# A middle q load on ScalarE's queue, and a new order of turns and copies in the first attention

## The chip, the cores and the metric

The kernel runs on one core of a Trainium2 chip. The metric is the device time of one execution in microseconds; of several executions the median is given. A profiled execution has a time of its own, and a span: the time from its first to its last instruction.

## What is computed

An attention with normalised q and k, for 8 batches of 12 heads, 448 positions and a head dimension of 64, and behind it a two-layer network with a tanh GELU (768 to 2048 to 768) over the 8 x 448 = 3584 rows. All inputs and the output are float32 in memory; the kernel multiplies in bfloat16.

```python
def rmsnorm(x, g):
    return x / np.sqrt(np.mean(x * x, axis=-1, keepdims=True) + 1e-06) * g
q_n, k_n = rmsnorm(q, g_q), rmsnorm(k, g_k)
scores = q_n @ k_n.transpose(0, 1, 3, 2) / np.sqrt(64)
attn = softmax(scores)                       # over the keys
x = (attn @ v).transpose(0, 2, 1, 3).reshape(3584, 768)
out = gelu_tanh(x @ w_in) @ w_out
```

## The kernel before

**Tiles.** Twelve heads are taken in three groups of four, here the first, middle and last group of a batch (c = 0, 1, 2; `NCH` is 3). The two head pairs of a group lie side by side. A q or k tile of a group (`rawq`, `rawk`, loaded by `load`, L115) is 128 partitions x 2 x 7 x 64 float32, 448 KB; the 7 (`NT`) are pieces of 64 positions.

**From q and k to scores.** Five steps lie between a load and the scores: the square (`square`, L154, on ScalarE, GpSimd or VectorE), its sum over the 64 columns (`total`, L167, VectorE), the inverse root (`rsqrt`, L190: on ScalarE a logarithm at L195 and an exponential at L202, L211 or L214), the product with the tile (`normed`, L268, on GpSimd or VectorE), the transposes on TensorE, one for each piece (`turn`, L286), and the copy from PSUM to `qT` or `kT` (`put`, L296; for k times the gain). `t_first` stands for pieces 0 to 3 of a tile and `t_rest` for pieces 4 to 6, so each of these steps can be done in two parts.

**Units.** A unit (`unit`, L324) is one k piece of one group against all of that group's q: four matmuls into one of two PSUM buffers (L333), then one exponential of 128 x 896 on ScalarE (L337). A batch has 21 units; units 0 to 6 belong to the first group, 7 to 13 to the middle, and 14 to 20 to the last. Unit i needs `qT` of its group and the k piece i modulo 7, and its buffer must have been left by the exponential of unit i - 2.

**Products.** `products(b, c, what, lo, hi)` (L368) multiplies the exponentials of pieces lo to hi with ones (`what` 0, the sums of the softmax) or with v (`what` 1). For the first two groups of batch 0 both go to the same two PSUM banks (`oall`) one after the other, or the sums go to two spare banks (`spared`). `turned` (L390) moves the sums from PSUM by two 32x32 block transposes (tile `st`), `recips` (L395) takes reciprocals and spreads them by another one (`rb`), and `quad_x` (L404) multiplies the v products by them into `xT`, the network's input.

**Order.** Nothing is re-ordered by a scheduler: each engine works through its instructions in the order in which the program issues them. For batch 0 that order is written out by hand: `first_attention` (L580) runs the 21 units and issues behind unit i what the list `mid` (L732) holds under i, and ahead of unit i what `side` (L725) holds. `idle(2, warm())` (L263) issues two matmuls whose result nobody uses; they write into a bank of `oall`. Later batches mix the attention of batch b + 1 with the second layer of batch b; the change does not touch them.

**The start.** Loads of the first group are cut: half of q by SyncE's queue and half by ScalarE's, k in two parts (`t_first`, `t_rest`) by SyncE's. ScalarE then issues the small load of `g_k` (L626) and loads its table of functions (L627). The middle and the last group's q and k (L628, L629) and batch 1's loads follow on SyncE's queue in order. GpSimd norms the first pieces of the first q (L690), squares middle q and middle k (L694, L696), issues two loads of v, squares last q and k, and issues four loads of `w_in`. VectorE's `total` of the middle k is the last step before the logarithm of `rsqrt(0, 1)`, which ScalarE runs behind unit 2.

**PSUM tiles of pool `ps_m`.** It has two buffers that rotate: a third tile waits until the readers of the first are done. Targets of `turn`, the roots of the last group (`place`) and the spare banks come from it.

Of the kernel before, what the change touches and what calls it, by code (L numbers as in the profile page):

```python
# [8 lines left out]
F32 = mybir.dt.float32  # L9
# [8 lines left out]
def kernel(  # L18
# [11 lines left out]
    nc = tc.nc  # L30
    B, H, S, D = q.shape
# [6 lines left out]
    P = 128  # L38
# [13 lines left out]
    stp = ctx.enter_context(tc.tile_pool(name="stp", bufs=1))  # L52
    smp = ctx.enter_context(tc.tile_pool(name="smp", bufs=4))
# [16 lines left out]
    def pair(name):  # L70
        rounds.append(rounds.pop(0))
        return rounds[-1]

    def three():
        return len(rounds) == 3
# [24 lines left out]
    rows = consts.tile([D, P], BF16)  # L100
# [14 lines left out]
    def load(b, c, n, parts=1, engs=(nc.sync,)):  # L115
        t = rawqk.tile([P, 2, NT, D], F32, tag=f"raw{n}", name=f"raw{n}")
        src = {"q": q, "k": k}[n]
        raws[n, b, c] = t
        m = 2 // parts
        return [  # L120
            lambda i=i: engs[i].dma_start(
                t[:, i * m:(i + 1) * m].rearrange("p a t d -> p a (t d)"),
                src[b, 4 * c + 2 * i * m:4 * c + 2 * (i + 1) * m].rearrange(
                    "(a r) (p t) d -> (r p) a (t d)", r=2, t=NT
                ),
            )
            for i in range(parts)
        ]

    def loads(b, c):  # L130
        for n in "qk":
            for go in load(b, c, n):
                go()
# [15 lines left out]
    def squares(b, c, n, hs, ts):  # L149

        sq = sqs[n, b, c]
        return sq[hs.start][:, :, ts] if type(sq) is list else sq[:, hs, ts]
# [10 lines left out]
    def seat(b, c):  # L163

        return (0, 2, 1)[c] if b == 1 else c

    def total(b, c, n, hs=both, ts=slice(0, NT)):  # L167
        if b not in sss:
            sss[b] = smp.tile([P, NCH, 2, 2, NT], F32, tag="ss", name="ss")
        nc.vector.reduce_sum(  # L170
            sss[b][:, seat(b, c), "qk".index(n), hs, ts], squares(b, c, n, hs, ts), axis=AX.X
        )
# [90 lines left out]
    def idle(n, w):  # L263

        for _ in range(n):
            nc.tensor.matmul(w, filler[:, :128], filler, start=True, stop=True)  # L266

    def normed(b, c, n, eng, ts=slice(0, NT)):  # L268
        if (n, b, c) not in nrms:
            nrms[n, b, c] = nrmp.tile([P, NT, 2, D], BF16, tag=f"nrm{n}", name=f"nrm{n}")  # L270
        m = ts.stop - ts.start
        root = rinvs[b][:, seat(b, c), "qk".index(n)] if eng is nc.gpsimd else roots[n, b, c]
        eng.tensor_mul(  # L273
            nrms[n, b, c][:, ts].rearrange("p t a d -> p a t d"),
            raws[n, b, c][:, :, ts],
            root[:, :, ts].to_broadcast([P, 2, m, D]),
        )

    def qT_of(b):
        if b not in qT:  # L280
            qT[b] = qkp.tile([128, NCH, NT, 2, R], BF16, tag="qT", name="qT")
        return qT[b]
# [3 lines left out]
    def turn(b, c, n, ts=slice(0, NT)):  # L286

        if ts.start == 0 and ts.stop == NT:
            tps[n] = ps_m.tile([128, 1024], BF16, tag="mm", name="tp")
        for t in range(ts.start, ts.stop):  # L290
            nc.tensor.transpose(  # L291
                tps[n][:, t * 128:(t + 1) * 128],
                nrms[n, b, c][:, t].rearrange("p a d -> p (a d)"), ident,
            )

    def put(b, c, n, ts=slice(0, NT), eng=nc.vector):  # L296
        dst = (kT if n == "k" else qT_of(b))[:, c, ts]
        src = tps[n][:, :TR].rearrange("p (t r s) -> p t r s", r=2, s=R)[:, ts]
        if n == "k":
            nc.vector.tensor_scalar(dst, src, gcol[:, 0:1], None, op0=ALU.mult)  # L300
        elif eng is nc.scalar:
            nc.scalar.copy(dst, src)
        else:
            nc.vector.tensor_copy(dst, src)
# [17 lines left out]
    exs, ess, oas = {}, {}, {}  # L322
# [45 lines left out]
    def products(b, c, what, lo=0, hi=NT):  # L368

        if lo == 0 and three():  # L370
            o = oas["o", what] = pair("o")
            oas[what] = [o[:, r, :S] for r in range(2)]
        elif lo == 0:
            oas[what] = spare.pop() if spare else [o[:, :S] for o in oall]
        o = oas[what]
        es = [exs[b, c][:, t] for t in range(NT)]
        if not what and added(b, c):
            es[:added(b, c) + 1] = [ess[b, c]]
        n = len(es)
        for i in range(lo, min(hi, n)):  # L380
            for r in range(2):
                rs = slice(r * R, (r + 1) * R)
                for a in range(2):
                    nc.tensor.matmul(  # L384
                        o[r][a * D:(a + 1) * D],
                        vb[b % 2][rs, 2 * c + a, i] if what else ones[rs], es[i][rs, a],
                        start=(i == 0), stop=(i == n - 1),
                    )

    def turned():  # L390
        st = oas["st"] = stp.tile([128, 2, S // 32, 32], F32, tag="st", name="st")
        for r in range(2):
            nc.vector.transpose(st[:, r].rearrange("p a b -> p (a b)"), oas[0][r])  # L393

    def recips():  # L395

        rb = oas["rb"] = stp.tile([128, 2, S], F32, tag="rb", name="rb")
        rc = smp.tile([128, 2 * S // 32], F32, tag="rc", name="rc")
        nc.vector.reciprocal(rc, oas["st"].rearrange("p r a b -> p (r a) b")[:, :, 0])
        nc.vector.transpose(  # L400
            rb.rearrange("p r s -> p (r s)"), rc.to_broadcast([128, 2 * S // 32, 32])
        )

    def quad_x(b, c):  # L404
        if c == 0:
            xT[b] = xp.tile([128, HP, S], BF16, tag="xT", name="xT")
        if three():
            nc.vector.tensor_mul(
                xT[b][:, 2 * c:2 * c + 2], oas["o", 1][:, :, :S], oas["rb"]
            )  # L410
            return
        for r in range(2):
            nc.vector.tensor_mul(xT[b][:, 2 * c + r], oall[r][:, :S], oas["rb"][:, r])
# [199 lines left out]
    t_first, t_rest = slice(0, 4), slice(4, NT)  # L613
# [11 lines left out]
        go()  # L625
    load_g(1, g_k, nc.scalar)  # L626
    nc.scalar.preload_act_table_set(EXP_SET)  # L627
    loads(0, 1)  # L628
    loads(0, 2)  # L629

    nc.vector.memset(eps, 1e-6)
    for i in range(3):
        nc.vector.memset(ones[:, i * D // 4:(i + 1 + i // 2) * D // 4], 1.0)
    for i in range(3):
        nc.vector.memset(
            rows[:, i * P // 4:(i + 1 + i // 2) * P // 4], (D ** 0.5) * (1 + 2.0 ** -7)
        )

    free = g.rearrange("p f s -> p (f s)")
    for i, (n, b, c) in enumerate((("q", 0, 1), ("k", 0, 1), ("q", 0, 2),  # L640
# [20 lines left out]
    def warm():  # L661
        return oall[0][:, :S]
# [39 lines left out]
    for j in range(2):  # L702
        rs = slice(j * 32, (j + 1) * 32)
# [18 lines left out]
    for a in range(2):  # L722
# [2 lines left out]
    side = [(1, lambda: loads(1, 0)),  # L725
            (2, lambda: loads(1, 2)),
            (7, lambda: loads(1, 1))]
    def turn_rest():
        tps["k"] = ps_m.tile([128, 1024], BF16, tag="mm", name="tp")
        turn(0, 0, "k", t_rest)  # L730

    mid = [(0, lambda: idle(2, warm())),  # L732
           (1, turn_rest, lambda: idle(2, warm())),
           (2, lambda: rsqrt(0, 1, near=(0, 1)), lambda: idle(2, warm())),
           (3, lambda: put(0, 0, "k", t_rest), lambda: normed(0, 1, "q", nc.vector),
            lambda: normed(0, 1, "k", nc.vector, t_first),
            lambda: normed(0, 1, "k", nc.vector, t_rest), lambda: idle(2, warm())),
           (4, lambda: idle(2, warm())),
           (5, lambda: turn(0, 1, "q"), lambda: put(0, 1, "q")),
           (6, lambda: turn(0, 1, "k"), lambda: put(0, 1, "k", t_first),  # L740
            lambda: put(0, 1, "k", t_rest)),
           (7, lambda: total(0, 2, "q"), lambda: total(0, 2, "k"),
            lambda: products(0, 0, 0, 0, 3)),
           (8, lambda: products(0, 0, 0, 3), lambda: turned(),
            lambda: rsqrt(0, 2, near=(1,)), lambda: normed(0, 2, "q", nc.gpsimd),
            lambda: normed(0, 2, "k", nc.vector, t_first),
            lambda: normed(0, 2, "k", nc.vector, t_rest), lambda: recips(),
            lambda: square(1, 0, "q", nc.gpsimd), lambda: w_in_part(1, 2),
            lambda: square(1, 0, "k", nc.gpsimd),
            lambda: w_out_part(0), lambda: load_v(1, 0, HP),  # L750
            lambda: square(1, 2, "q", nc.gpsimd), lambda: square(1, 2, "k", nc.gpsimd),
            lambda: w_out_part(1)),
           (9, lambda: idle(2, warm())),
           (10, lambda: products(0, 0, 1, 0, 3)),
           (11, lambda: products(0, 0, 1, 3)),
           (12, lambda: turn(0, 2, "q"), lambda: put(0, 2, "q"), lambda: turn(0, 2, "k"),
            lambda: put(0, 2, "k", t_first), lambda: put(0, 2, "k", t_rest),
            lambda: quad_x(0, 0)),

           (14, lambda: spared(), lambda: products(0, 1, 0, 0, 4)),  # L760
           (15, lambda: products(0, 1, 0, 4), lambda: turned(), lambda: recips()),
# [134 lines left out]
```

## Time and profile before

| | |
|---|---|
| Median of three runs | 404.31 us (404.3, 404.31, 408.4) |
| Profiled execution, its own time | 405.4 us |
| Profiled execution, span | 403.6 us |
| TensorE busy | 393.4 us (97%) |
| ScalarE busy | 281.0 us (70%) |
| VectorE busy | 257.7 us (64%) |
| GpSimd busy | 123.0 us (30%) |
| Granted TensorE clock | 0.999 of full speed |

In the rows of the profile PE is TensorE, ACT is ScalarE, DVE is VectorE, POOL is GpSimd and SP is SyncE; a q behind the name (SPq, ACTq) marks the issue of a DMA. A row of the timeline has the start in us from the span's start, the busy time, the engine, the line, the operation, the tile written and the tile read with their shapes, and the number of instructions that were merged into the row. In brackets stands the idle time of that engine just ahead of it, and what ended it. The row of an exponential names the tile `ex`, that of a unit's scores the tile `t`; transposes write `tp`. A row of the DMA view has the size of one transfer and the time from its issue to its landing. Busy times of matmuls are modelled, since they overlap.

### The profile page before, as it was taken

To read this page: it belongs to the slowest core of one execution; us is meant where nothing else is said; L and a number is where in the kernel's file an instruction comes from. 1 tells how busy PE (TensorE), PEld (TensorE's weight loads), DVE (VectorE), ACT (ScalarE), POOL (GpSimd) and SP (SyncE) were. 2 spreads that over 40 slices of the span, in tenths; PEclk is the share of its full clock that TensorE was granted. 3 is DMA by queue.
4 is the path that set the end of the run, shared out by engine and by line. 5 is a ranking of instruction groups with operands and counts; after the bars stand their busy time and mean duration, and the time that the engine had idled before them with its cause. 6 is when DMAs were issued, how large, how long until landed. Compare 5 with 4: busy or idle time off the path is not lost.

```text
span 403.6 us, 8096 instructions
## 1 busy us (share of the span) xinstructions
PE 393.4 (97%) x3321; PEld 209.8 (52%) x3321; DVE 257.7 (64%) x436; ACT 281.0 (70%) x382; POOL 123.0 (30%) x103
## 2 busy tenths in 40 slices
PE   7799999999999999999999999999999999999996
PEld 3365555555555555554555555555555545555564
DVE  5998858985796369845699357963698405990010
ACT  6995498868974887847975689748878359744301
POOL 4993407364007230093004540072301800000000
PEclk9999999999999999999999999999999999999999
DMA  8999995998515954169612938139413511110033
GB/s 280 312 212 208 200 211 210 239 233 228 97 41 105 256 97 143 41 162 288 107 41 63 255 60 221 40 85 275 69 41 80 115 24 39 50 47 24 2 78 80
DMA packets 65561, 54.07 MB, mean 134 GB/s; under 512 B 37364, under 2 KB 60532, under 8 KB 65524
## 3 DMA queue, kind: packets, MB, share of 16 engines
q1 hardware_dynamic: 53184, 41.48, 38.3%
q0 software_dynamic: 12112, 11.80, 18.8%
q8 instruction: 26, 0.43, 0.4%
q10 hardware_dynamic: 228, 0.28, 0.3%
q14 instruction: 11, 0.09, 0.1%
HBM read 45.61 MB, written 11.01 MB: 140 GB/s over the span
## 4 chain that ended last, share of the span: by engine, by line
PE 94%; ACT 2%; DMA 2%; POOL 1%; DVE 0%; SPq 0%; issue 0%
PE o L443 38%; PE h L422 24%; PE t L473 12%; PE t L333 9%; PE t L384 8%; ACT ex L337 2%; DMA rawq<-in_q_dram 2%; PE o L384 1%; POOL g L161 1%; PE tp L291 1%; SPq L617 0%; PE os L384 0%; DVE st L393 0%; DVE ss L170 0%; PE o L266 0%
## 5 line engine op out<-in xcount | busy, mean ns | idle before, releaser
L337 ACT ACTIVATE ex<-t,shift 128x896 bf16<-128x896 f32 x168 | 157.6, 1005 | 22.0 <-PE t L333 19.4
L443 PE MATMUL o<-wout,g 128*128 128x384 bf16 (+1 forms) x912 | 156.8, 324 | 0.0
L443 PEld LDWEIGHTS <-g 128*128 128x128 bf16 x912 | 83.6, 98 | 67.7 <-issue 18.8
L422 PE MATMUL h<-xT,win 128*128 128x448 bf16 x516 | 99.1, 352 | 0.0
L170 DVE TENSOR_REDUCE ss<-sq 128x14 f32<-128x896 f32 (+3 forms) x45 | 44.3, 999 | 49.1 <-ACT sq L159 46.1
L422 PEld LDWEIGHTS <-win 128*128 128x128 bf16 x516 | 50.5, 98 | 47.1
L428 ACT ACTIVATE g<-h 128x448 bf16<-128x448 f32 x86 | 46.6, 543 | 28.2 <-PE h L422 23.1
L453 DVE COPY osb<-o 128x384 f32<-128x384 f32 x41 | 22.7, 554 | 52.6 <-PE o L443 50.6
L333 PE MATMUL t<-qT,kT 64*64 64x448 bf16 x672 | 47.0, 359 | 3.0 <-DVE kT L300 1.0
L473 PE MATMUL t<-xT,win 128*128 128x448 bf16 x252 | 49.6, 352 | 0.0
L478 ACT ACTIVATE g<-t 128x896 bf16<-128x896 f32 x21 | 18.4, 915 | 33.0 <-PE t L473 33.0
L666 POOL COPY mark<-es 1x1 bf16<-1x1 bf16 x6 | 1.1, 177 | 131.5 <-DVE es L355 131.5
L273 POOL TENSOR_TENSOR nrmq<-rawq,rinv 128x896 bf16<-128x896 f32 (+1 forms) x21 | 34.8, 1658 | 12.0 <-DVE o L236 7.7
L473 PEld LDWEIGHTS <-win 128*128 128x128 bf16 x252 | 24.5, 98 | 22.8 <-issue 0.6
L273 POOL TENSOR_TENSOR nrmk<-rawk,rinv 128x896 bf16<-128x896 f32 x20 | 33.5, 1679 | 0.0
L333 PEld LDWEIGHTS <-kT 64*64 64x64 bf16 x672 | 17.4, 105 | 28.1 <-issue 20.8
L384 PE MATMUL t<-ex,vb 64*64 64x448 bf16 x588 | 31.6, 350 | 0.0
L451 ACT COPY osb<-o 128x384 f32<-128x384 f32 (+1 forms) x16 | 7.3, 458 | 31.5 <-PE o L443 31.5
L400 DVE STREAM_TRANSPOSE rb<-rc 128x896 f32<-128x896 f32 x24 | 26.7, 1111 | 0.8
L358 DVE TENSOR_TENSOR e<-ex 128x896 bf16<-128x896 bf16 x33 | 20.0, 607 | 9.7 <-ACT ex L337 9.4
L384 PEld LDWEIGHTS <-vb 64*64 64x64 bf16 x672 | 20.4, 107 | 11.1 <-issue 2.4
L393 DVE STREAM_TRANSPOSE st<-t 128x448 f32<-128x448 f32 x42 | 24.6, 625 | 1.0 <-PE t L384 0.9
(93 smaller groups left out, 294.5 us busy)
## 6 DMA issues: line engine op xcount, KB each, us to landing
out_dram<-osb SPq DMA_DIRECT2D x54, 192.0 KB, 2.7
rawq<-in_q_dram SPq DMA_DIRECT2D x23, 448.0 KB, 4.3
rawk<-in_k_dram SPq DMA_DIRECT2D x23, 448.0 KB, 5.5
vb<-in_v_dram POOLq DMA_DIRECT2D x7, 672.0 KB, 6.7
win<-in_moe_w_in_dram POOLq DMA_DIRECT2D x8, 384.0 KB, 11.0
wout<-in_moe_w_out_dram POOLq DMA_DIRECT2D x2, 1536.0 KB, 24.0
vb<-in_v_dram POOLq DMA_DIRECT2D x1, 448.0 KB, 10.5
qT<-nrmq SPq DMA_TRANSPOSE x19, 4.9
```

The costliest lines, as they stand in the source:

```text
L170: nc.vector.reduce_sum(sss[b][:, seat(b, c), "qk".index(n), hs, ts], squares(b, c, n, hs, ts), axis=AX.X)
L273: eng.tensor_mul(nrms[n, b, c][:, ts].rearrange("p t a d -> p a t d"), raws[n, b, c][:, :, ts], root[:, :, ts].to_broadcast([P, 2, m, D]),)
L333: nc.tensor.matmul(sc[r * R:(r + 1) * R, a, :S], kT[rs, c, t, r], qT[b][rs, c, :, r], start=True, stop=True,)
L337: nc.scalar.activation(ex[:, t], sc[:, :, :S], AF.Exp, scale=scale, bias=shift)
L384: nc.tensor.matmul(o[r][a * D:(a + 1) * D], vb[b % 2][rs, 2 * c + a, i] if what else ones[rs], es[i][rs, a], start=(i == 0), stop=(i == n ...
L393: nc.vector.transpose(st[:, r].rearrange("p a b -> p (a b)"), oas[0][r])
L400: nc.vector.transpose(rb.rearrange("p r s -> p (r s)"), rc.to_broadcast([128, 2 * S // 32, 32]))
L422: nc.tensor.matmul(h[:, :S], win[:, c, f * 128:(f + 1) * 128], xT[b][:, c], start=(c == 0), stop=(c == HP - 1),)
L428: nc.scalar.activation(g[:, f, (b % 2) * S:(b % 2 + 1) * S], h[:, :S], AF.Gelu_apprx_tanh)
L443: nc.tensor.matmul(o, g[:, f, i * 128:(i + 1) * 128], wout[:, f, lo:hi], start=(f == 0), stop=(f == nf - 1),)
L453: nc.vector.tensor_copy(osb[:, lo:hi], o)
L473: nc.tensor.matmul(h[:, j, :S], win[:, c, f * 128:(f + 1) * 128], xT[b][:, c], start=(c == 0), stop=(c == HP - 1),)
```

## The change

The middle q of batch 0 is loaded by ScalarE's queue, behind `g_k` and the table load; SyncE's queue loses that one load. A constant (`rows`) is filled in two pieces, not in three.

In the first attention the order changes:

- The middle k's first four pieces are turned right behind the middle q, after unit 5, into a tile of their own, and put at once. Its last three pieces are normed behind unit 8 (after the products with ones), turned and put behind unit 9, where two idle matmuls stood.
- The sums of the last group's squares are issued behind unit 6, and not behind unit 7.
- The last k is normed behind unit 9 and turned behind unit 11, one unit sooner, ahead of the last q, and between the fourth and fifth piece of the first group's products with v; the products of pieces 5 and 6 come behind unit 13.
- `recips` is divided: `recip` takes all reciprocals behind unit 9, and `spread` spreads them in two halves, one behind unit 11 and one behind unit 12.
- `quad_x(0, 0)` moves from unit 12 to unit 13.

```diff
--- before.py
+++ after.py
@@ -392,14 +392,23 @@
         for r in range(2):
             nc.vector.transpose(st[:, r].rearrange("p a b -> p (a b)"), oas[0][r])
 
+    def recip():
+
+        oas["rb"] = stp.tile([128, 2, S], F32, tag="rb", name="rb")
+        rc = oas["rc"] = smp.tile([128, 2 * S // 32], F32, tag="rc", name="rc")
+        nc.vector.reciprocal(rc, oas["st"].rearrange("p r a b -> p (r a) b")[:, :, 0])
+
+    def spread(rs=slice(0, 2)):
+        m = S // 32
+        rc = oas["rc"][:, rs.start * m:rs.stop * m]
+        nc.vector.transpose(
+            oas["rb"][:, rs].rearrange("p r s -> p (r s)"),
+            rc.to_broadcast([128, (rs.stop - rs.start) * m, 32]),
+        )
+
     def recips():
-
-        rb = oas["rb"] = stp.tile([128, 2, S], F32, tag="rb", name="rb")
-        rc = smp.tile([128, 2 * S // 32], F32, tag="rc", name="rc")
-        nc.vector.reciprocal(rc, oas["st"].rearrange("p r a b -> p (r a) b")[:, :, 0])
-        nc.vector.transpose(
-            rb.rearrange("p r s -> p (r s)"), rc.to_broadcast([128, 2 * S // 32, 32])
-        )
+        recip()
+        spread()
 
     def quad_x(b, c):
         if c == 0:
@@ -625,16 +634,16 @@
         go()
     load_g(1, g_k, nc.scalar)
     nc.scalar.preload_act_table_set(EXP_SET)
-    loads(0, 1)
+
+    for go in load(0, 1, "q", 1, (nc.scalar,)) + load(0, 1, "k"):
+        go()
     loads(0, 2)
 
     nc.vector.memset(eps, 1e-6)
     for i in range(3):
         nc.vector.memset(ones[:, i * D // 4:(i + 1 + i // 2) * D // 4], 1.0)
-    for i in range(3):
-        nc.vector.memset(
-            rows[:, i * P // 4:(i + 1 + i // 2) * P // 4], (D ** 0.5) * (1 + 2.0 ** -7)
-        )
+    for i in range(2):
+        nc.vector.memset(rows[:, i * P // 2:(i + 1) * P // 2], (D ** 0.5) * (1 + 2.0 ** -7))
 
     free = g.rearrange("p f s -> p (f s)")
     for i, (n, b, c) in enumerate((("q", 0, 1), ("k", 0, 1), ("q", 0, 2),
@@ -725,37 +734,37 @@
     side = [(1, lambda: loads(1, 0)),
             (2, lambda: loads(1, 2)),
             (7, lambda: loads(1, 1))]
-    def turn_rest():
+    def turn_new(c, ts):
         tps["k"] = ps_m.tile([128, 1024], BF16, tag="mm", name="tp")
-        turn(0, 0, "k", t_rest)
+        turn(0, c, "k", ts)
 
     mid = [(0, lambda: idle(2, warm())),
-           (1, turn_rest, lambda: idle(2, warm())),
+           (1, lambda: turn_new(0, t_rest), lambda: idle(2, warm())),
            (2, lambda: rsqrt(0, 1, near=(0, 1)), lambda: idle(2, warm())),
            (3, lambda: put(0, 0, "k", t_rest), lambda: normed(0, 1, "q", nc.vector),
-            lambda: normed(0, 1, "k", nc.vector, t_first),
-            lambda: normed(0, 1, "k", nc.vector, t_rest), lambda: idle(2, warm())),
+            lambda: normed(0, 1, "k", nc.vector, t_first), lambda: idle(2, warm())),
            (4, lambda: idle(2, warm())),
-           (5, lambda: turn(0, 1, "q"), lambda: put(0, 1, "q")),
-           (6, lambda: turn(0, 1, "k"), lambda: put(0, 1, "k", t_first),
-            lambda: put(0, 1, "k", t_rest)),
-           (7, lambda: total(0, 2, "q"), lambda: total(0, 2, "k"),
-            lambda: products(0, 0, 0, 0, 3)),
-           (8, lambda: products(0, 0, 0, 3), lambda: turned(),
+           (5, lambda: turn(0, 1, "q"), lambda: put(0, 1, "q"),
+            lambda: turn_new(1, t_first), lambda: put(0, 1, "k", t_first)),
+           (6, lambda: total(0, 2, "q"), lambda: total(0, 2, "k")),
+           (7, lambda: products(0, 0, 0, 0, 3)),
+           (8, lambda: products(0, 0, 0, 3), lambda: normed(0, 1, "k", nc.vector, t_rest),
+            lambda: turned(),
             lambda: rsqrt(0, 2, near=(1,)), lambda: normed(0, 2, "q", nc.gpsimd),
-            lambda: normed(0, 2, "k", nc.vector, t_first),
-            lambda: normed(0, 2, "k", nc.vector, t_rest), lambda: recips(),
             lambda: square(1, 0, "q", nc.gpsimd), lambda: w_in_part(1, 2),
             lambda: square(1, 0, "k", nc.gpsimd),
             lambda: w_out_part(0), lambda: load_v(1, 0, HP),
             lambda: square(1, 2, "q", nc.gpsimd), lambda: square(1, 2, "k", nc.gpsimd),
             lambda: w_out_part(1)),
-           (9, lambda: idle(2, warm())),
+           (9, lambda: turn(0, 1, "k", t_rest), lambda: put(0, 1, "k", t_rest),
+            lambda: normed(0, 2, "k", nc.vector, t_first),
+            lambda: normed(0, 2, "k", nc.vector, t_rest), lambda: recip()),
            (10, lambda: products(0, 0, 1, 0, 3)),
-           (11, lambda: products(0, 0, 1, 3)),
-           (12, lambda: turn(0, 2, "q"), lambda: put(0, 2, "q"), lambda: turn(0, 2, "k"),
-            lambda: put(0, 2, "k", t_first), lambda: put(0, 2, "k", t_rest),
-            lambda: quad_x(0, 0)),
+           (11, lambda: products(0, 0, 1, 3, 5), lambda: turn(0, 2, "k"),
+            lambda: put(0, 2, "k", t_first), lambda: spread(slice(0, 1))),
+           (12, lambda: turn(0, 2, "q"), lambda: put(0, 2, "q"),
+            lambda: put(0, 2, "k", t_rest), lambda: spread(slice(1, 2))),
+           (13, lambda: products(0, 0, 1, 5), lambda: quad_x(0, 0)),
 
            (14, lambda: spared(), lambda: products(0, 1, 0, 0, 4)),
            (15, lambda: products(0, 1, 0, 4), lambda: turned(), lambda: recips()),
```

## The prediction, made before the changed kernel ran

> **What bounds the kernel now.** I read the busy time by stretch first, then the chain that ended last, then ScalarE's and VectorE's timelines of the first 31 us, and the DMA rows last.
>
> ```profile
> 0.00:31.50 31.50, 25.01 (x326) 13.81 (x327) 24.18 (x50) 26.95 (x41) 25.93 (x34) 1.00 1.02 266
> 31.50:350.00 318.50, 318.50 (x2636) 167.33 (x2636) 219.56 (x366) 235.31 (x314) 97.08 (x70) 1.00 0.60 136
> 350.00:403.60 53.60, 49.91 (x363) 28.65 (x360) 14.00 (x22) 18.71 (x29) 0.00 (x0) 0.99 0.18 45
> ```
>
> The first number after the stretch's length is TensorE's busy time. From 31.5 to 350 us it is 318.50 of 318.50: no hole. So whatever the change does in the first attention, which ends near 31.5 us, reaches the end of the span one for one, and only the first 31.5 us are open. The chain names what rules them:
>
> ```profile
> 2.20 6.35 DMA rawq<-in_q_dram
> ...
> 31.50 3.13 PE t L473 x16
> ```
>
> The piece at 2.20 is the load of the middle q: issued by SyncE at 2.20, landed at 8.55. ScalarE, whose 21 exponentials (one for each unit) are the long row of this stage, shows what follows from it:
>
> ```profile
> 0.74 0.40 ACTq L121 DMA_DIRECT2D rawq<-in_q_dram  x1
> 1.19 1.10 ACTq L86 DMA_DIRECT2D grow<-in_g_k_dram  x1
> 2.32 1.28 ACT L627 ACT_TABLE_LOAD   x1 [2.32 <-POOL ident masks.py:197]
> 4.12 1.05 ACT L159 ACTIVATE sq<-rawq 128x448 f32<-128x448 f32 x2 [0.52 <-DMA rawq<-in_q_dram]
> ...
> 9.20 2.80 ACT L337 ACTIVATE ex<-t,shift 128x896 bf16<-128x896 f32 x3
> 12.77 0.32 ACT L195 ACTIVATE lg<-ss,eps 128x28 f32<-128x28 f32 x1 [0.77 <-DVE ss L170]
> 13.12 0.20 ACT L211 ACTIVATE o<-lg 128x28 f32<-128x28 f32 x1
> 13.25 3.68 ACT L337 ACTIVATE ex<-t,shift 128x896 bf16<-128x896 f32 x4
> 17.09 1.90 ACT L337 ACTIVATE ex<-t,shift 128x896 bf16<-128x896 f32 x2 [0.15 <-PE t L333]
> 18.94 0.32 ACT L195 ACTIVATE lg<-ss,eps 128x28 f32<-128x28 f32 x1
> ...
> 19.51 4.82 ACT L337 ACTIVATE ex<-t,shift 128x896 bf16<-128x896 f32 x5
> ```
>
> From 9.20 on ScalarE has few holes: 0.77 us before the logarithm at 12.77 (the middle pair's root), 0.15 us before unit 7 at 17.09, and some 0.2 us inside the last row:
>
> ```profile
> 22.22 2.12 ACT L337 ACTIVATE ex<-t,shift 128x896 bf16<-128x896 f32 x2
> ```
>
> Two exponentials took 1.90 at 17.09 and 2.12 here: 0.22 us in which unit 13 was waited for. The sum, 0.77 + 0.15 + 0.22 = 1.14, is an estimate of the most that any order of this stage can win while the exponentials keep their length and the first starts at 9.20.
>
> **Part 1, middle q by ScalarE's queue.** Removed: one issue on SyncE; the middle k and all later loads there go out one place earlier:
>
> ```profile
> 2.71 0.47 SPq L121 DMA_DIRECT2D rawk<-in_k_dram  x1
> ```
>
> so k at 2.20 in place of 2.71. Added: one issue on ScalarE, behind the table load, which ends at 2.32 + 1.28 = 3.60. ScalarE is then idle until its first square at 4.12 (the 0.52 in brackets), and an issue takes 0.40 to 0.47: free to within 0.1 us. If this one takes 1.10 like the row at 1.19, the square starts 0.6 us late; three exponentials later ScalarE stands 0.77 us idle, and that covers it.
>
> How soon does q land? The first q gives the only pair of loads that share the two queues:
>
> ```profile
> rawq<-in_q_dram SPq DMA_DIRECT2D x1, 224.0 KB, 3.4
> rawq<-in_q_dram ACTq DMA_DIRECT2D x1, 224.0 KB, 3.2
> ```
>
> Both went out at 0.74 and landed together, so the queues move side by side. Issued at 3.65, the first 224 KB would be there after 3.2 us at 6.85, and the other 224 KB (0.23 MB) at half of the rate of that time:
>
> ```profile
> 5.00:8.50 3.50, 1.57 (x16) 0.77 (x14) 3.35 (x8) 2.99 (x10) 1.78 (x4) 1.00 1.00 357
> rawk<-in_k_dram SPq DMA_DIRECT2D x1, 448.0 KB, 7.0
> ```
>
> 0.23 MB at 357/2 GB/s is 1.28 us: landed at 8.1, an estimate, against 8.55. Ends: 7.1 if the rest comes at the full rate, 10.65 if it takes k's 7.0 us (second row) from 3.65. I take 8.1, nearest to the pair of rows. The middle k lands at 2.71 + 7.0 = 9.7 as before: the same bytes lie ahead of both together. The remainder of the first k shares its time with q and may come some tenths late; the hole of 0.77 us covers that too.
>
> Here the Trainium skill speaks against the change: "DMA: Bandwidth & Descriptors", Issuing engines are not separate DMA queues, says that issuing from several engines saves only the sequencer's time, since all run on the same 16 DMA engines; by that alone q would come 1.45 us later with its issue, and the sum would be the slower rival below. The same page, Queues, rings and completion order, says that each DMA engine goes round between the queues that have work, which is the even sharing of the pair of rows above; by that the sum is mine.
>
> GpSimd squares q and k in turn:
>
> ```profile
> 6.60 1.04 POOL L273 TENSOR_TENSOR nrmq<-rawq,rinv 128x512 bf16<-128x512 f32 x1 [0.55 <-POOL gbf L676]
> 8.62 1.68 POOL L161 TENSOR_TENSOR g<-rawq 128x896 f32<-128x896 f32 x1 [0.98 <-DMA rawq<-in_q_dram]
> 10.26 1.82 POOL L161 TENSOR_TENSOR g<-rawk 128x448 f32<-128x448 f32 x2
> ```
>
> With q at 8.1 its square starts at 8.16, and k's at 9.80 in place of 10.26, just behind k's landing at 9.7. Both limits give 0.46 us; an earlier q would not add to it while k stays. The last sum, the logarithm (12.77 to 12.31) and unit 3 (13.25 to 12.79) follow by 0.46. ScalarE is free at 12.00, so 0.3 of its 0.77 us stays.
>
> **Part 2, the order.** VectorE is as full as ScalarE here; these rows give the durations:
>
> ```profile
> 14.36 1.14 DVE L273 TENSOR_TENSOR nrmk<-rawk,o 128x512 bf16<-128x512 f32 x2
> 15.42 0.62 DVE L304 COPY qT<-tp 128x896 bf16<-128x896 bf16 x1
> 16.11 0.81 DVE L300 TENSOR_SCALAR kT<-tp,gcols 128x512 bf16<-128x512 bf16 x2
> ...
> 18.82 1.17 DVE L393 STREAM_TRANSPOSE st<-o 128x448 f32<-128x448 f32 x2
> 19.92 1.11 DVE L273 TENSOR_TENSOR nrmk<-rawk,root 128x512 bf16<-128x512 f32 x2
> 20.95 0.31 DVE L399 RECIPROCAL rc<-st 128x28 f32<-128x28 f32 x1
> 21.30 1.11 DVE L400 STREAM_TRANSPOSE rb<-rc 128x896 f32<-128x896 f32 x1
> ```
>
> Unit 7, the first of the middle pair, waits for what it needs of the row at 16.11 (TensorE's rows; the second is seven transposes):
>
> ```profile
> 16.65 0.38 PE L333 MATMUL t<-qT,kT 64*64 64x448 bf16 x4 [0.58 <-DVE kT L300]
> ...
> 22.00 0.56 PE L291 MATMUL tp<-ident,nrmq 128*128 128x128 bf16 x7
> ```
>
> *Up to unit 7.* The change takes the second half of the k norm (about half of 1.14) from ahead of the q copy, and the last three k transposes and their copy from ahead of unit 7. VectorE's first k half then ends near 14.5 (14.36 - 0.46 + 0.57), q's transposes about 14.72; the q copy starts at 14.76 (was 15.42), k's first piece follows at 15.3 and ends at 15.78, and unit 7's scores can start at 15.83 (was 16.65). Now ScalarE limits it: the four exponentials before hold it until 12.79 + 3.68 = 16.47, of which the last 0.1 overlaps the next (13.25 + 3.68 is 16.93, and the 0.15 us in brackets is counted from there): 16.36. So unit 7's exponential goes from 17.09 to 16.36: 0.46 by the queue, and 0.27 by the order.
>
> *To unit 9.* The two sums of the last pair (1.9 us, from the copy's end at 16.92 to 18.82) start at 15.7 and end by 17.7. The logarithm follows its two exponentials by 1.85 us (17.09 to 18.94), at 18.2, when the sums are there, and unit 9 comes 0.57 us behind it (18.94 to 19.51), at 18.78: 0.73 gained. The k half norm now stands between the sums and st: st starts at 18.14 (was 18.82) and ends at 19.31.
>
> *Units 10 and 11.* In place of the two idle matmuls stand three transposes that wait for that norm until 18.27. Unit 10 is queued behind them: its scores come at 18.6 to 19.0, and its exponential is due one later than unit 9's, at 19.68: hidden. The put of k's last three pieces comes behind st, 19.24 to 19.65, so unit 11 starts at 19.9 and ends at 20.3; its exponential is due at 20.58: hidden by 0.25.
>
> *Units 12 to 15.* The last k's norm runs 19.56 to 20.70, its seven transposes follow (0.56, most of them before the norm's second half ends), and unit 12 is queued behind them on TensorE: scores 21.0 to 21.4, exponential due at 21.48. This is the tightest place of the new order: free now, and each tenth that the norm slips is a tenth lost (0 to 0.15). Half a spread (0.56 of 1.11; two halves cost some 0.06 more) moves behind the q put, so the q copy is done at 22.7 and unit 14 is in time. The sums behind unit 14 write into a bank that the last put must first leave, at 23.0; sixteen products later unit 15 ends at 24.33, which sets its exponential at 24.35. Before, it is the second behind the pair at 22.22: 22.22 + 2.12 - 0.1 for the overlap, and 0.95 (a fifth of 4.82) for unit 14, some 25.2. No later wait replaces the 0.22 us.
>
> **The sum.** 0.46 (queue) + 0.27 (unit 7) + 0.1 (what is left of the 0.22 at unit 13) = 0.83 at unit 15, which I round to 0.8. Everything later keeps its distance, and TensorE passes it on. Where the cover is thinnest (unit 12) it is 0.65; if middle k also lands by 9.2, its issue's 0.5 us earlier, it is up to 1.14. The profiled execution took 405.4 us for its span of 403.6, so it would take 404.6; the median of the runs shown is 404.31, and 404.31 - 0.8 = 403.5.
>
> **The rivals.** *More:* middle k lands earlier too and the hole at 12.00 closes: 1.0 to 1.14, time 403.2. For it: k's earlier issue. Against: the bytes ahead of it are the same.
> *Order alone:* the queue brings nothing, q lands at 8.55 again. Unit 7 is then asked at 16.82 (0.27), and VectorE's lead at units 12 and 13 shrinks so that 0.3 is left: 404.0. For it: k's landing bounds GpSimd anyway.
> *Slower:* q, issued 1.45 us later, is served by its time of issue behind middle and last loads of SyncE. Landing 3.65 + 6.35 = 10.0 up to 10.65, its square, k's squares, the logarithm and unit 3 all come 1.4 to 2.1 us late; less the order's 0.3 that is 1.1 to 1.8 slower, 405.4 to 406.1. It decides from a landing of 8.55 + 0.3 = 8.9 on. For it: the 6.35 and 7.0 us of the loads behind a filled queue. Against: the pair of rows that landed together.
>
> **How the numbers follow.** Chances: mine (0.5 to 1.0 us gained, 403.3 to 403.8) 0.55, more 0.1, order alone 0.2, slower 0.15. The forecast is 403.5. The range runs from 402.8 (404.31 less 1.14, and 0.4 for runs that differ by a thousandth) to 404.8, past "order alone" and up to the near side of the slower case, leaving some 0.15 to 0.2 outside. One per cent is 4.04 us, about what a measurement of this kernel can tell from no change (the three runs shown reach from 404.3 to 408.4). No case moves the time that far: the gain is bounded by the 1.14 us of holes and the worst slower case is 2: within 1% 0.97, faster 0.01, slower 0.02.
>
> **What would show it.** Queue: GpSimd's first square of the middle q starts at 8.2 or sooner, without the 0.98 us wait, and k's at 9.8; the hole before ScalarE's logarithm is 0.3. Order: no wait before unit 7's exponential, which starts near 16.4; unit 9's near 18.7; no hole before units 11, 12 and 13; from unit 15 on every exponential begins 0.8 us sooner, and TensorE has no new hole behind 31 us. Wrong would be: the middle q landing after 8.9; ScalarE's first square well after 4.2 with no hole left to take it; a wait of ScalarE for unit 12; or a hole of TensorE after 31 us, through which a gain in the first attention would be lost.

## The result and the profile after

The changed kernel took 407.06 us (median of 22 runs, 404.61 to 411.31), the kernel before beside it 404.52 us (22 runs, 404.17 to 408.4). The ratio is 1.0046, 95% interval [1.0031, 1.0062]: 1.9 us slower. It leaves out one slow run of 411.31 us and is taken over the runs, not from the two medians, which lie 2.5 us apart. The forecast was 403.5, with a range up to 404.8. The profiled execution of the changed kernel took 408.43 us with a span of 406.6 us, 3.0 us more than the span of before. It lies near the upper end of the 22, so it shows the mechanisms, and somewhat too much of their size.

The same three stretches as before, busy time by engine, TensorE's behind the length of the stretch:

```profile
0.00:31.50 31.50, 24.67 (x299) 13.39 (x303) 23.35 (x49) 25.24 (x40) 24.10 (x33) 1.00 0.97 250
31.50:350.00 318.50, 316.78 (x2640) 166.27 (x2632) 217.50 (x362) 235.66 (x313) 98.96 (x71) 1.00 0.62 137
350.00:406.70 56.70, 52.92 (x389) 30.16 (x386) 16.87 (x27) 20.11 (x31) 0.00 (x0) 1.00 0.17 43
```

Two things are new. The first stretch holds less TensorE work than before (299 matmuls against 326), so the first attention is late. And the second stretch, which was full, has a hole of 1.72 us. The chain that ended last names a load for each:

```profile
2.37 7.93 DMA rawq<-in_q_dram
...
34.30 31.16 DMA wout<-in_moe_w_out_dram
```

The first piece is the middle q again: issued at 2.37, landed at 10.30 (8.55 before). ScalarE's timeline shows the issue, and what the late landing does:

```profile
2.34 1.28 ACT L636 ACT_TABLE_LOAD   x1 [2.34 <-POOL ident masks.py:197]
2.37 0.39 ACTq L121 DMA_DIRECT2D rawq<-in_q_dram  x1
3.92 1.04 ACT L159 ACTIVATE sq<-rawq 128x448 f32<-128x448 f32 x2 [0.30 <-DMA rawq<-in_q_dram]
...
8.68 0.52 ACT L159 ACTIVATE sq<-rawk 128x384 f32<-128x384 f32 x1 [1.86 <-DMA rawk<-in_k_dram]
...
10.54 2.81 ACT L337 ACTIVATE ex<-t,shift 128x896 bf16<-128x896 f32 x3
14.52 0.32 ACT L195 ACTIVATE lg<-ss,eps 128x28 f32<-128x28 f32 x1 [1.18 <-DVE ss L170]
14.87 0.20 ACT L211 ACTIVATE o<-lg 128x28 f32<-128x28 f32 x1
15.00 5.48 ACT L337 ACTIVATE ex<-t,shift 128x896 bf16<-128x896 f32 x6
20.34 0.35 ACT L195 ACTIVATE lg<-ss,eps 128x28 f32<-128x28 f32 x1
...
20.95 11.18 ACT L337 ACTIVATE ex<-t,shift 128x896 bf16<-128x896 f32 x12
```

The table load runs from 2.34 to 3.62, and the issue at 2.37 lies beside it, not behind it. The first exponential is at 10.54 (9.20 before), since the first k's last pieces came late and held ScalarE for 1.86 us. But the middle logarithm at 14.52 (12.77 before) waited another 1.18 us: the late first exponentials were covered, and the middle pair sets the time. Behind the logarithm there is no hole any more: six exponentials in one row, where before 0.15 us stood ahead of unit 7, and twelve in another. GpSimd shows why the logarithm is late:

```profile
6.39 1.05 POOL L273 TENSOR_TENSOR nrmq<-rawq,rinv 128x512 bf16<-128x512 f32 x1 [0.59 <-POOL gbf L685]
10.37 1.68 POOL L161 TENSOR_TENSOR g<-rawq 128x896 f32<-128x896 f32 x1 [2.93 <-DMA rawq<-in_q_dram]
12.01 1.82 POOL L161 TENSOR_TENSOR g<-rawk 128x448 f32<-128x448 f32 x2
```

It waited 2.93 us for q, where it had waited 0.98. The loads of that time, with their times from issue to landing, in two answers of the DMA view (issues at 1.7; at 2.19 for k and 2.37 for q):

```profile
rawk<-in_k_dram SPq DMA_DIRECT2D x1, 192.0 KB, 7.0
```

```profile
rawk<-in_k_dram SPq DMA_DIRECT2D x1, 448.0 KB, 8.5
rawq<-in_q_dram ACTq DMA_DIRECT2D x1, 448.0 KB, 7.9
```

Middle k lands at 10.7 and middle q at 10.3: nearly together. Before, q came at 8.55 and k 1.2 us behind it. The first k's last pieces landed at 8.65, 6.3 before. The last new wait is TensorE's, at the second half of `wout`:

```profile
65.51 1.14 PE L452 MATMUL o<-wout,g 128*128 128x384 bf16 x6 [1.72 <-DMA wout<-in_moe_w_out_dram]
```

The network's first matmul, before and after:

```profile
31.44 3.20 PE L473 MATMUL t<-xT,win 128*128 128x448 bf16 x16
```

```profile
32.89 2.44 PE L482 MATMUL t<-xT,win 128*128 128x448 bf16 x12
```

So the 3.0 us divide into 1.45 us ahead of the network and 1.55 us behind its start, where the hole at 65.51 is the only new one.

### The profile page after: what moved, and what is told of

The parts are those of the page before. It is cut to its first block, busy times and chain, and to the rows that moved or that the text cites. A ratio compares the mean times of both kernels' runs of the same rounds, so it can differ in the third digit from the quotient of the medians.

```text
span 406.6 us, 8095 instructions
## 1 busy us (share of the span) xinstructions
PE 394.4 (97%) x3319; PEld 209.8 (52%) x3319; DVE 257.7 (63%) x436; ACT 281.0 (69%) x382; POOL 123.1 (30%) x103
## 4 chain that ended last, share of the span: by engine, by line
PE 83%; DMA 12%; POOL 3%; issue 0%; ACT 0%; POOLq 0%; ACTq 0%
PE o L452 35%; PE h L431 23%; PE t L384 8%; PE t L333 8%; PE t L482 8%; DMA wout<-in_moe_w_out_dram 8%; DMA win<-in_moe_w_in_dram 3%; DMA rawq<-in_q_dram 2%; POOL g L161 2%; POOL vb L144 1%; POOL sq L161 0%; POOL grow L86 0%; POOL win L662 0%; ACT osb L460 0%; POOL ident masks.py:197 0%
## 5 line engine op out<-in xcount | busy, mean ns | idle before, releaser
L482 PEld LDWEIGHTS <-win 128*128 128x128 bf16 x252 | 24.5, 98 | 22.6 <-issue 0.4
L404 DVE STREAM_TRANSPOSE rb<-rc 128x896 f32<-128x896 f32 (+1 forms) x25 | 26.8, 1073 | 0.8
L417 DVE TENSOR_TENSOR xT<-t,rb 128x896 bf16<-128x896 f32 x21 | 22.9, 1089 | 5.2 <-PE t L384 4.4
```

The lines of the kernel that those rows point to most:

```text
L404: nc.vector.transpose(oas["rb"][:, rs].rearrange("p r s -> p (r s)"), rc.to_broadcast([128, (rs.stop - rs.start) * m, 32]),)
L417: nc.vector.tensor_mul(xT[b][:, 2 * c:2 * c + 2], oas["o", 1][:, :, :S], oas["rb"])
L482: nc.tensor.matmul(h[:, j, :S], win[:, c, f * 128:(f + 1) * 128], xT[b][:, c], start=(c == 0), stop=(c == HP - 1),)
```

## The experiments

The first theory, Q: the queue did the harm, and the order helps a little. Its rival, O: the order did it. Each kernel was compared with the kernel before on the same chip.

**Order alone.** `e1_order_only` is the changed kernel with

```diff
-    for go in load(0, 1, "q", 1, (nc.scalar,)) + load(0, 1, "k"):
-        go()
+    loads(0, 1)
```

> Theory Q (the queue did the harm, the order helps): with the middle q back on SyncE's queue, the first k's last pieces land near 6.3 us again and the middle q near 8.6; ScalarE's square of the first k's last pieces starts near 7.0 and not at 8.7; the first matmul of the network starts at 31.1 (31.43 before, 32.89 in the changed kernel); no wait for wout at 65 us; ratio to before 0.999. Rival O (the new order did the harm): ratio 1.003 to 1.005, the first network matmul near 32.5.

Measured: 0.9994 [0.9969, 1.0018], best run 403.85 (404.14 of the 33 of before). Its GpSimd and ScalarE:

```profile
8.72 1.68 POOL L161 TENSOR_TENSOR g<-rawq 128x896 f32<-128x896 f32 x1 [1.14 <-DMA rawq<-in_q_dram]
```

```profile
12.87 0.32 ACT L195 ACTIVATE lg<-ss,eps 128x28 f32<-128x28 f32 x1 [0.93 <-DVE ss L170]
```

q lands at 8.65 (8.55 before), the logarithm is 0.1 us behind that of before, and the network's first matmul (31.25) 0.2 us ahead: O falls.

**Queue alone.** `e2_queue_only` is the kernel before with the reverse edit.

> Theory Q: with the old order and the middle q on ScalarE's queue, ScalarE waits over 1 us for the first k's last pieces, the middle q lands after 9.5 us, the first network matmul starts at 33.2 (0.3 later than in the changed kernel) and there is a wait for wout near 65 us of 1.5 us or more; ratio to before 1.005. Rival O: ratio 1.000, the first network matmul at 31.4.

Measured: 1.0034 [1.0012, 1.0055], with the old order. So the queue is the harm, by itself or by what follows from it. But only part of the expectation held: q landed at 8.84, not after 9.5; ScalarE did not wait for the first k's last pieces, and there was no wait for `wout`. The late first k of the changed kernel's profile is not the cause; in a profile of the order alone (e10, below), which lost nothing, it was 1.3 us late too. The network's first matmul was late all the same (34.05), and these rows of ScalarE, and of TensorE, show another cost:

```profile
13.06 0.32 ACT L195 ACTIVATE lg<-ss,eps 128x28 f32<-128x28 f32 x1 [1.28 <-DVE ss L170]
...
18.45 1.01 ACT L337 ACTIVATE ex<-t,shift 128x896 bf16<-128x896 f32 x1 [1.01 <-PE t L333]
```

```profile
14.94 0.93 PE L291 MATMUL tp<-ident,nrmq 128*128 128x128 bf16 x7
```

Seven transposes took 0.93 us, where 0.56 is usual: the granted clock had fallen (the last section).

**The first k's last pieces by ScalarE's queue instead.** `e3_k_rest_by_act` is the order alone, with

```diff
-        lambda ts=ts: nc.sync.dma_start(
+        lambda ts=ts: (nc.sync if ts.start == 0 else nc.scalar).dma_start(
```

> New order, the middle q on SyncE's queue, and the first k's last pieces on ScalarE's queue ahead of the small load. Theory Q: these pieces land before 6.3 us and the middle q, issued 0.5 us sooner, near 8.1, so the hole before the logarithm of the middle pair shrinks by 0.3 to 0.5 us; first network matmul at 30.7; ratio 0.998. If landings are set by the bytes alone and not by the place in the queue, the same as the order alone: 31.1, ratio 0.999. Rival O: 1.003 or more.

Measured: 1.001 [0.9995, 1.0026]; first network matmul at 31.41. The pieces landed in time and q at 7.8, but nothing was won, for a small load stood in the way:

```profile
6.90 0.57 POOL L683 TENSOR_TENSOR gprod<-grow 64x32 f32<-64x32 f32 x2 [4.27 <-DMA grow<-in_g_k_dram]
```

`g_k` (0.2 KB) went out behind those pieces on the same queue and came just ahead of 6.9; GpSimd's first norm, which TensorE needs, stood behind it.

**wout earlier.** `e4_wout_early` is the changed kernel with GpSimd's list of unit 8 re-ordered:

```diff
-            lambda: w_out_part(0), lambda: load_v(1, 0, HP),
+            lambda: w_out_part(0), lambda: load_v(1, 0, HP), lambda: w_out_part(1),
             lambda: square(1, 2, "q", nc.gpsimd), lambda: square(1, 2, "k", nc.gpsimd),
-            lambda: w_out_part(1)),
```

> The changed kernel, with the second half of wout issued by GpSimd ahead of two squares, 3.3 us sooner. Theory W (the wait at 65 us follows from the late issue): the wait of 1.72 us goes, TensorE has no hole after 31 us, and the time is 1 to 1.7 us under that of the changed kernel, ratio to before 1.001 to 1.003. Rival (the rate of the loads of weights sets the landing, not the issue): the wait stays within 0.5 us of 1.72, ratio 1.0045.

Measured: 1.004 [1.0014, 1.0065]. TensorE had no hole after 31 us, yet the time can't be told from the changed kernel's. Issued at 30.49 the second half landed at 62.0; in the kernel before it was issued at 32.47 and landed at 61.4. So W was right on the hole and not on the time. Set against the kernel before, 2 us of earlier issue brought no earlier landing, and the hole of 1.72 us belongs to one profile (the changed kernel's second one, below, has none) and is no part of the median that this edit could find.

What was left was q's late landing itself. Theory S: two loads that stand side by side on two queues end together, so the one that is needed first becomes late. Rival L: a load by ScalarE's queue is late by itself. Theory G: a fallen clock is a second cost.

**Idle matmuls in the hole.** `e5_fill` is the changed kernel with `idle(8, warm())` for `idle(2, warm())` behind unit 3.

> The changed kernel with eight idle matmuls, not two, ahead of unit 4 (behind unit 3), where TensorE stands idle for 1.3 us and more. Theory G (the halved clock is a second cost: TensorE's idle time before unit 4 lets the granted clock fall): of the changed kernel's 22 runs 13 had a mean clock of 0.997 or less; here at most 2 of 12; the median falls by 0.5 to 1.0 us against the changed kernel beside it. Rival (the clock only follows the lateness and costs nothing): share of low clocks unchanged, or fewer and the median the same.

Measured: 1.0026 [1.0003, 1.005], median 406.61; the changed kernel beside it (e8, below) had 406.62. Low clocks fell from 7 of 12 to 1 of 12, the median did not move. The ratio is 0.0016 (0.65 us) under that of e8, which is within the intervals. So the median speaks against G and does not settle it; the table below says more. The profile is that of the one run with a low clock, and the first cause is large in it:

```profile
14.57 0.32 ACT L195 ACTIVATE lg<-ss,eps 128x28 f32<-128x28 f32 x1 [2.73 <-DVE ss L170]
```

**Middle k held back.** `e6_k_behind_q` is the changed kernel, with SyncE's middle k and last loads behind VectorE's first sum:

```diff
-    for go in load(0, 1, "q", 1, (nc.scalar,)) + load(0, 1, "k"):
+    for go in load(0, 1, "q", 1, (nc.scalar,)):
         go()
-    loads(0, 2)
...
         total(0, 0, "q", slice(a, a + 1))
+        if a == 0:
+            for go in load(0, 1, "k"):
+                nc.vector.memset(raws["k", 0, 1][:1, 0, 0, :1], 0.0)
+                go()
+            loads(0, 2)
```

> The changed kernel, but SyncE issues the middle k (and the last loads behind it) only when VectorE has made the first sum of the first q, near 5.4 us, so that the middle q has ScalarE's queue with little beside it. Theory S (two loads side by side end together; the middle q is late because the middle k shares with it): q lands by 7.6 us, GpSimd squares it without a wait, the first k's last pieces land near 6.3, the middle k still by 10, the logarithm at 12.4 or sooner, the first network matmul near 30.8, ratio 0.998 to 0.999. Rival L (a load by ScalarE's queue is late by itself): q lands after 8.6 us, the logarithm after 12.8, ratio 1.002 or more.

GpSimd's rows:

```profile
7.49 1.68 POOL L161 TENSOR_TENSOR g<-rawq 128x896 f32<-128x896 f32 x1 [0.19 <-DMA rawq<-in_q_dram]
10.08 1.82 POOL L161 TENSOR_TENSOR g<-rawk 128x448 f32<-128x448 f32 x2 [0.91 <-DMA rawk<-in_k_dram]
```

The same q, on the same queue and issued at 2.35 (2.37 in the changed kernel), landed at 7.42: L falls, and S holds for the landing. But k, held back to 5.01, came only at 9.95, so the logarithm (12.59) gained little on that of before, and the time was 1.0029 [1.0006, 1.0052], not the 0.998 expected. The profiled run, with 405.56 us, had a full clock. 8 of the 12 runs had a low one, with a median of 407.5 us; the other four had 405.3. What lowered the clock in them was not traced.

**Order with wout earlier.** `e7_order_wout` is the order alone with the edit of `wout`; `e8_changed_again` is the changed kernel once more, beside it.

> The order alone (middle q on SyncE's queue) with the second half of wout issued ahead of two squares. If the landing of wout takes back what the order gains, TensorE's hole near 62 us is gone and the ratio is 0.998; if not, the same as the order alone: 0.999 to 1.000, best runs near 403.9.

> The changed kernel once more, beside the others. Theory Q: the middle q lands between 8.8 and 10.3 us (later than the 8.55 of before), GpSimd waits for it over 1 us, the logarithm comes after 13.0; the first k's last pieces are late in some profiles only (8.65 in the first one, 6.5 to 6.7 in two others with the same loads). Ratio 1.004 to 1.005, at least a third of the runs with a mean clock of 0.997 or less.

Measured: e7 0.9977 [0.9955, 0.9999], median 404.07; e8 1.0042 [1.0015, 1.007], q landed at 9.16, the logarithm at 13.38, 7 of 12 clocks low, all as expected. In e7's profile q landed at 7.58, which no edit of it explains, so it was run again, with the parts of it alone:

**wout alone, the order alone and both.** `e9_before_wout` is the kernel before with the edit of `wout`, `e10_order_again` is e1, `e11_order_wout_again` is e7.

> The kernel before with only the second half of wout issued ahead of two squares. Theory W (a thin margin of wout's landing near 62 us costs the kernel before too, in some runs): ratio 0.998 to 0.9995, fewer runs above 405 us than of the kernel before beside it. Rival: ratio 1.000, the same spread.

> The order alone once more, beside the next kernel: ratio 0.9995, best runs near 403.9; from the logarithm of the middle pair to the network's first matmul 18.4 us (18.66 before).

> The order with the earlier wout once more: ratio 0.998. If wout takes back a part of the order's gain, this is under the order alone by 0.2 to 0.6 us in the median of the same call; if the first measurement only had lucky landings, both are the same.

Measured: 1.0003 [0.9986, 1.002], 1.0002 [0.9986, 1.0017] and 0.9998 [0.9984, 1.0011]. None of the three differs from the kernel before, and e7's 0.9977 did not come again, though e7 and e11 are the same kernel; it is best read as luck. From the logarithm to the network's first matmul e10 took 18.37 us, as expected. The edit of `wout` does nothing that can be measured. e11's profile shows where a gain goes: q landed at 7.5, the logarithm came without a wait at 11.74, the network's first matmul at 30.11, 1.3 us sooner than before, and then

```profile
61.68 1.14 PE L452 MATMUL o<-wout,g 128*128 128x384 bf16 x6 [0.67 <-DMA wout<-in_moe_w_out_dram]
```

half of it was lost to `wout`, which had gone out at 29.24 and landed at 61.6 (61.4 in the kernel before).

**Middle k, not q, on ScalarE's queue.** `e12_k_by_act` is e11 with

```diff
-    loads(0, 1)
+    for go in load(0, 1, "k", 1, (nc.scalar,)) + load(0, 1, "q"):
+        go()
```

> The order with the earlier wout, and the middle k (not q) on ScalarE's queue; q stays on SyncE's queue, where it was. Theory S (two loads side by side end together): q lands after 8.7 us although its own queue and issue are those of before, the logarithm at 13.0 or later, ratio 1.002 to 1.004, that is 1.5 us or more over the kernel without it. Rival L (what rides on ScalarE's queue is late): q lands at 8.6 or sooner, only k late.

Measured: 1.0038 [1.0018, 1.0057], median 406.24, 1.7 us above e11, which ran beside it.

```profile
9.03 1.68 POOL L161 TENSOR_TENSOR g<-rawq 128x896 f32<-128x896 f32 x1 [1.63 <-DMA rawq<-in_q_dram]
```

q had its old queue and its old issue at 2.18 and landed at 8.96, with k at 9.37, 0.4 us behind it and not 1.2. L asked for q at 8.6 or sooner. The landing alone would be weak evidence against it, since q came as late as 8.87 from one queue (e10, below); but k came together with q, and the median shows that the harm is back with q on its old queue. So what harms q is that k stands beside it and not behind it. That is S again, by another edit.

The profiles side by side, in us (q, k: landing of the middle pair; "hole": TensorE's idle time before unit 4; "to network": from the logarithm to the network's first matmul; "half": how long the granted clock was 0.50 between 14 and 22 us; "low": runs with a mean granted clock of 0.997 or less). e3 and e6, with other loads, are left out; they had 5 and 8 low runs of 12.

| kernel | middle pair on | q | k | logarithm | hole | to network | half | low | ratio |
|---|---|---|---|---|---|---|---|---|---|
| before | one queue | 8.55 | 9.76 | 12.77 | 0.91 | 18.67 | 0 | 9 of 102 | 1 |
| e1 | one | 8.65 | 9.87 | 12.87 | 1.07 | 18.38 | 0 | 1 of 12 | 0.9994 |
| e10 (as e1) | one | 8.87 | 10.05 | 13.09 | 0.96 | 18.37 | 0 | 0 of 12 | 1.0002 |
| e7 | one | 7.58 | 8.74 | 11.79 | 0.28 | 18.38 | 0 | 2 of 12 | 0.9977 |
| e11 (as e7) | one | 7.52 | 8.71 | 11.74 | none | 18.37 | 0 | 2 of 12 | 0.9998 |
| e9 | one | 8.22 | 9.42 | 12.44 | 0.53 | 18.66 | 0 | 1 of 12 | 1.0003 |
| changed | two | 10.30 | 10.67 | 14.52 | 1.32 | 18.37 | 0 | 13 of 22 | 1.0046 |
| e8 (as changed) | two | 9.16 | 8.87 | 13.38 | 1.78 | 19.42 | 3.4 | 7 of 12 | 1.0042 |
| e4 | two | 9.35 | 9.03 | 13.56 | 1.89 | 19.14 | 3.4 | 6 of 10 | 1.004 |
| e5 | two | 10.36 | 9.75 | 14.57 | 1.72 | 19.33 | 3.4 | 1 of 12 | 1.0026 |
| e2 | two | 8.84 | 8.66 | 13.06 | 1.42 | 20.99 | 6.8 | 5 of 12 | 1.0034 |
| e12 | two | 8.96 | 9.37 | 13.18 | 1.56 | 20.62 | 6.8 | 4 of 9 | 1.0038 |

On one queue k lands 1.2 us behind q in each profile; on two they land within 0.6 us of each other. The later of the two comes at about the same time either way: 8.7 to 10.05 on one, 8.84 to 10.67 on two. On average q comes 1.3 us later on two queues (9.5 against 8.2), and k no sooner (9.4 and 9.4). So the two queues bring nothing forward; they only hold q back.

The table also shows that the low clock costs time of its own. With a full clock the way from the logarithm to the network took the same time in each profile, 18.37 or 18.38 us with the new order and 18.66 or 18.67 with the old one (e9, before). In the five profiles with a stretch at half clock it took 0.8 to 2.3 us more. Those five are the ones in which TensorE's hole before unit 4 was 1.42 us or longer; in the other seven it was 1.32 us at most. That a late q opens this hole and the hole brings the low clock fits these rows and e5's count, but no run shows it by itself.

## Why the prediction was wrong

- **q's issue.** "Behind the table load", at 3.65: wrong, it went out at 2.37 beside it. Earlier than assumed, so this error alone would have helped.
- **q's landing, the step that failed.** "The first 224 KB would be there after 3.2 us ... and the other 224 KB at half of the rate": 8.1 was forecast, 10.30 measured (8.84 to 10.36 in the five profiles with q on ScalarE's queue and k beside it). With the true issue at 2.37 that sum would even have given 6.85. The even sharing was seen rightly, from the first q's two halves. It was applied to half of the load, and the other half got the time of a transfer with nothing ahead of it. Those halves began the program; here the first k, and the middle k issued at 2.19, shared with all 448 KB. One end of the stated landings is a slip as well: at the full rate, 357 GB/s, the rest takes 0.64 us, which gives 7.5 and not 7.1. The consequence that mattered was not drawn: with even sharing the middle q and k must end together, so q has to come later than from a queue where it goes first. That is what the table shows: 9.5 us on average in place of 8.2.
- **The first k "some tenths late".** 2.3 us in the changed kernel's profile, 0.2 to 0.8 in the five others with the pair on two queues. In the changed kernel's profile it cost nothing: the hole of 1.18 us before the logarithm was still open.
- **GpSimd, logarithm, unit 3.** The chain was right, only its direction was not: q's square at 10.37 puts the logarithm 4.15 us later, at 14.52; before it was 4.15 as well (8.62 to 12.77).
- **The order.** Right nearly to the tenth. From the logarithm to unit 9 it forecast 6.47 us (12.31 to 18.78); measured 6.43 (14.52 to 20.95), 6.74 before. The 0.37 us for the order were 0.30: from the logarithm to the network's first matmul 18.37 (14.52 to 32.89) against 18.67. The tight place at unit 12 cost nothing: the row of twelve exponentials has no hole. A gain of 0.3 us is 0.0007 and below what these comparisons can tell (0.9994 and 1.0002 for the order alone).
- **"TensorE passes it on."** Wrong in both directions. A late landing of `wout` (65.5 us, 61.4 before) opened a hole of 1.72 us in one profile, and an early first attention met `wout`'s landing near 62 us in others (0.8 us lost in e6, 0.67 in e11). The rows of before had no hole there, and I took that for slack.
- **The rivals.** "Slower" (0.15) came nearest: 405.4 to 406.1 for a landing of 10.0 to 10.65. It is near the measured 1.9 us, though 407.06 lies above it; its mechanism, service by time of issue, is not what was found: q went out only 0.17 us later than before and landed 1.75 us later. The Trainium skill, "DMA: Bandwidth & Descriptors", Queues, rings and completion order, has the engines go round between the queues with work; the trace agrees, with q and k landing 0.4 us apart, and the sum by that rule is where I went wrong. The same page of the Trainium skill, Issuing engines are not separate DMA queues, has the better conclusion: no time but the issue's is saved.
- **What the sum did not have.** The granted clock had no term. An estimate from the table for the 1.9 us: the logarithm comes 1.3 us later on average on two queues (13.7 against 12.4), of which the order takes back 0.3; and 0.8 to 2.3 us of half clock in 13 of 22 runs are 0.5 to 1.4 us more. Together that is 1.5 to 2.4 us. How the loss divides in one run stays open, and e5, which removed most of the low clocks, did not lower the median. But among the runs of the kernel before too, those with a low clock had a median near 406.7 us and the others 404.6.

## What to carry to other kernels

Two loads that are needed one after the other belong on one queue in that order: on two queues they shared the rate here, and the first one came about as late as the second. Before a load is moved, write down for each load near it when it is needed, and give the rate to the one that is waited for. And a stretch without holes does not prove slack: look for the landing that is nearest to its use before a gain is passed through.

## What the runs showed of the hardware

- A DMA issue of ScalarE does not wait for its table load: the load at 2.34 took 1.28 us, the issue came at 2.37, in the changed kernel and in e2 and e6 alike (2.36 and 2.35).
- The granted clock can halve in the first attention. In e2, by stretch (the third number from the right, ahead of the DMA share, is the clock):

```profile
11.40:14.80 3.40, 1.68 (x16) 0.56 (x12) 2.95 (x6) 2.09 (x5) 3.38 (x5) 1.00 1.07 366
14.80:21.60 6.80, 6.22 (x62) 3.10 (x58) 4.58 (x8) 5.07 (x8) 4.88 (x7) 0.50 1.16 265
```

  After a stretch of 3.4 us in which TensorE was busy for 1.68 us, by the modelled ends, the clock was 0.50 for 6.8 us. The Trainium skill, "TensorE: Matmul & The Clock Gate", Part 1: The HAM clock gate, puts a halved clock down to an idle window of some 3.4 us; here that stretch was half busy. In the changed kernel's own profile a stretch with 1.60 us (8.0 to 11.4) had no such effect; no run shows what decides between the two.
- `wout`'s second half (1536 KB) took 24.5 to 32.6 us to land in the fourteen profiles. Issued between 27.9 and 30.5 it landed at 59.6 to 62.0 us (five profiles), issued between 32.0 and 32.5 at 59.7 to 62.6 (five), later still at 58.8 to 65.5 (four): an issue 2 or 3 us sooner brought no clearly earlier landing.
